# A new order for all operations of a banded attention kernel with a gated output, and its dummy products in pairs

## The chip, the core and the metric

The kernel runs on one core of one Trainium2 chip. The core has five engines that work side by side and each take their own instructions strictly in the order in which the program gives them: TensorE (PE: matrix products; its weight loads are listed apart as PEld), VectorE (DVE), ScalarE (ACT), GpSimd (POOL) and SyncE (SP), whose queue here issues the loads and nearly all stores. They wait for each other through semaphores. The metric is device time in microseconds. Three runs of the kernel before took 269.23, 270.71 and 270.84 us (median 270.71); the profiled execution took 267.36 us, 265.6 us of it between its first and its last instruction (the span).

## What is computed

```python
B, H, S, D = 4, 8, 768, 64; n_sink, window = 4, 128; KT = 5
scores = q @ k.T / sqrt(D)                      # per batch and head
keep   = (key < n_sink) | (0 <= query - key < window)
a      = softmax(where(keep, scores, -1e9))     # row maximum taken off first
x      = (a @ v), heads side by side            # [B, S, 512]
gate   = sigmoid(sum_k conv_w[k] * x[s - 4 + k])   # causal, 5 taps, per channel
out    = (gate * (x @ w_val)) @ w_out
```

The three weights of the second half come as 64-bit floats, which the kernel takes apart itself, as bits, into pairs of 32-bit numbers (a high and a low half); the products of that half are each made from three products of such halves.

## The kernel before, in words

The sequence is cut into 24 steps: 4 batches, 3 blocks of 256 queries, 2 groups of four heads. Steps 0, 1, 6, 7, 12, 13, 18 and 19 are the first blocks of their batches. Two steps (both head groups of one block) make a pair m = 0 to 11, for which the second half is computed. Every piece of work is a named event, `name.step`, and one table of these names, `ORDER`, sets the order in which all engines get their instructions. The function `banded` walks through the table and calls each event. The queues are in order, so the table is the schedule. The names that are spoken of here:

- `kq.s`, `vv.s`: loads of K and Q, and of V, on SP's queue (L234 to L247); three buffers each. `wvl.c`, `wol.c`: loads of a quarter of w_val or w_out, 512 KB (L331); `wva` to `wvf`, `woa` to `wof`: the six stages that take it apart (ACT L135, L149, L154, L181; DVE L138 to L163; POOL L155, L167; for w_val also PE L176 to L178).
- `s0.s`, `s1.s`: the scores of two heads (PE L373) with the mask and the row maximum (DVE L378, and L382 or, in first blocks, L387). `e0`, `e1`: their exponentials (ACT L397). `rec`: one over the row sum, with one instruction on ACT (L403) and one on DVE (L404). `norm`: the normalising (POOL L412 to L421). `tx`, `sk`: transposes on PE (L434, L439). `px` (DVE L463), `py` (ACT L471), `ts` (L447 or L449): they empty the transposes' PSUM.
- `vl.s`, `si.s`: the product with V and that with the sink rows (PE L491, L500), both into the one PSUM tile `xv`. `xc`, `xh`, `hd` (ACT L507, L515, L519): two copies of it, and the 4 columns at its head that the taps reach back to. `xl` (POOL L523): the low half. `c4` (POOL L528), then `c0`, `c1` (DVE L536, four instructions each): the five taps. `vl` of the next step writes `xv` again and waits for `xc`, `xh`, `c0` and `c1`. `th`: the gate's tanh (ACT L541).
- `v0` to `v3` (12 products each, PE L555): x @ w_val in four column blocks, two to a PSUM bank. `y0`, `y1` (ACT L561) copy such a bank out for m = 0 and 1. `g`, `h`, `l` (DVE L574, ACT L580, POOL L584): gate times value, its high half, its low half. `o0` to `o3` (six products each, PE L606): the product with w_out. `t0`, `t1` (ACT L612, then a store): one block of 128 rows to HBM. In the last pair `o2.11` and `o3.11` write their two column halves into two banks, and `t1.11` stores them apart, the second on ACT's own queue.
- `fill`: dummy products of zeros (PE L222), 128 by 512. They write a bank that is free at that point; nothing reads them.

PSUM is tight. `s0`, `s1` and `tx` take turns on two pairs of banks (`pr`): each waits until the user before last has been read, by the exponentials, or in first blocks by DVE, or by `px` and `py`. The products `v`, `o`, `sk`, the w_val stage `wve` and the fills take turns on two banks (`ac`), each of which comes free when `g` (or `y`), `t`, `ts` or `wvf` has read it.

Of the kernel before, what the change touches and what calls it, by code (L numbers as in the profile page):

```python
# [41 lines left out]
sk.1 c1.0 wvf.2 wol.2 e1.3 ts.1 sk.2 px.2 vl.1 rec.3 th.0 woe.1 si.1 xc.1 xh.1 hd.1 wvd.3 s0.4 c4.1 wof.1 c0.1
fill.4g py.2 vv.10 wve.3 woa.2 ts.2 xl.1 woa.3 norm.3 e0.4 c1.1 s1.4 vv.2 wod.1 wvf.3 wob.2 v0.0 wob.3 v1.0 vv.5
tx.3 vl.2 vv.3 y0.0 th.1 v2.0 g0.0 hd.2 py.3 woe.3 h0.0 si.2 e1.4 l0.0 xc.2 v3.0 wod.3 o2.0 px.3 woe.2 y1.0 g1.0
c4.2 rec.4 kq.8 h1.0 wod.2 s0.6 xh.2 e0.6 wof.2 l1.0 s0.5 c0.2 o0.0 wof.3 c1.2 s1.6 o3.0 t1.0 e0.5 o1.0 xl.2 norm.4
sk.3 ts.3 vl.3 si.3 t0.0 kq.7 xc.3 xh.3 tx.4 hd.3 s1.5 sk.4 ts.4 px.4 e1.5 xl.3 v0.1 c4.3 v1.1 rec.5 py.4 v2.1 vv.4
c0.3 y0.1 th.2 c1.3 g0.1 e1.6 v3.1 y1.1 s1.7 s0.7 norm.5 th.3 vl.4 h0.1 l0.1 e1.7 si.4 tx.5 kq.9 rec.6 sk.5 xc.4
o0.1 kq.12 ts.5 g1.1 px.5 hd.4 s1.8 h1.1 o2.1 c4.4 l1.1 xh.4 c0.4 e0.7 o1.1 norm.6 xl.4 o3.1 t0.1 sk.6 vv.7 c1.4
rec.7 py.5 norm.7 tx.6 px.6 vl.5 e1.8 si.5 ts.6 t1.1 py.6 xh.5 xc.5 s0.9 s0.8 xl.5 vv.6 c4.5 sk.7 v0.2 hd.5 ts.7
th.4 e0.9 v1.2 sv.7 c0.5 v2.2 tx.7 c1.5 e0.8 rec.8 sv.6 g0.2 py.7 s1.9 px.7 v3.2 kq.10 th.5 vl.6 h0.2 s1.10 si.6  # L50
e1.9 norm.8 g1.2 xc.6 xh.6 hd.6 l0.2 rec.9 c4.6 tx.8 o0.2 vv.8 h1.2 l1.2 o2.2 xl.6 c0.6 py.8 c1.6 px.8 e1.10 o3.2
scalars s0.12 vl.7 s0.10 norm.9 si.7 t1.2 sk.8 xc.7 tx.9 xh.7 ts.8 hd.7 o1.2 e0.10 c4.7 xl.7 c0.7 v0.3 c1.7 vv.9
v1.3 kq.11 rec.10 vl.8 th.6 si.8 e0.12 px.9 th.7 g0.3 s0.11 xc.8 c4.8 v2.3 xh.8 t0.2 hd.8 py.9 h0.3 sk.9 v3.3 c0.8
vv.11 l0.3 c1.8 s1.11 ts.9 e0.11 g1.3 s1.12 e1.11 h1.3 vl.9 o0.3 norm.10 si.9 tx.10 hd.9 xl.8 l1.3 o2.3 xc.9 kq.13
px.10 rec.11 xh.9 c4.9 kq.15 kq.14 o3.3 e1.12 vv.13 c0.9 o1.3 c1.9 t1.3 sk.10 norm.11 py.10 t0.3 ts.10 s0.13 rec.12
vl.10 xl.9 vv.12 si.10 xh.10 xc.10 tx.11 c4.10 sk.11 hd.10 xl.10 v0.4 ts.11 px.11 th.9 c0.10 e0.13 py.11 sv.12
norm.12 v1.4 v2.4 th.8 c1.10 s1.13 vl.11 tx.12 si.11 g0.4 v3.4 px.12 e1.13 sk.12 rec.13 h0.4 g1.4 py.12 s0.14 xc.11
xh.11 hd.11 vv.16 l0.4 h1.4 c4.11 l1.4 e0.14 kq.18 warm_up s1.14 norm.13 e1.14 ts.12 o2.4 c0.11 o3.4 o0.4 c1.11
s1.18 s0.18 vl.12 si.12 tx.13 vv.18 kq.19 hd.12 th.10 py.13 o1.4 px.13 xl.11 s0.15 t0.4 s1.15 v2.5 t1.4 xc.12 sv.18
xh.12 sk.13 rec.14 c4.12 ts.13 th.11 c0.12 e1.18 c1.12 v3.5 norm.14 v0.5 kq.16 e0.15 e1.15 v1.5 sv.13 g0.5 s0.16  # L60
kq.17 g1.5 vl.13 tx.14 h0.5 si.13 l0.5 o2.5 h1.5 l1.5 xh.13 vv.14 hd.13 rec.15 xc.13 o0.5 c4.13 e0.16 th.12 px.14
o1.5 norm.15 py.14 c0.13 t0.5 o3.5 sk.14 c1.13 tx.15 ts.14 t1.5 py.15 px.15 s1.16 xl.12 vl.14 e0.18 s0.17 hd.14
xl.13 si.14 xc.14 sk.15 kq.20 v2.6 c4.14 xh.14 ts.15 e1.16 v3.6 v0.6 c0.14 rec.16 vv.15 xl.14 th.13 c1.14 e0.17 g1.6
v1.6 g0.6 s1.19 h0.6 norm.16 th.14 l0.6 s0.19 h1.6 kq.21 vl.15 s1.17 l1.6 rec.18 sk.16 si.15 xc.15 ts.16 xh.15 c4.15
tx.16 px.16 o0.6 hd.15 o1.6 c0.15 e1.17 c1.15 rec.17 t0.6 xl.15 py.16 e1.19 th.15 v0.7 v1.7 s0.20 norm.18 vl.16
si.16 xh.16 norm.17 g0.7 tx.17 xc.16 sk.18 v2.7 py.17 h0.7 v3.7 vv.17 c4.16 px.17 hd.16 ts.18 vv.20 c0.16 e0.19 o2.6
g1.7 c1.16 e0.20 h1.7 o3.6 sk.17 ts.17 rec.19 l0.7 kq.23 l1.7 s1.20 e1.20 s0.21 vl.17 o0.7 t1.6 si.17 tx.18 o1.7
norm.19 xc.17 xh.17 c4.17 px.18 hd.17 rec.20 vv.19 py.18 o2.7 c0.17 e0.21 t0.7 xl.16 o3.7 c1.17 tx.19 xl.17 th.17
vl.18 py.19 px.19 s1.21 norm.20 kq.22 si.18 th.16 t1.7 xc.18 tx.20 sk.19 vv.21 px.20 v0.8 c4.18 ts.19 hd.18 sv.19
c0.18 c1.18 v1.8 v2.8 e1.21 v3.8 g0.8 sk.20 py.20 flag ts.20 s1.22 g1.8 xh.18 vl.19 s0.22 h0.8 hd.19 l0.8 si.19 o0.8  # L70
xc.19 xl.18 h1.8 rec.21 c4.19 o2.8 l1.8 xh.19 vv.23 o3.8 c0.19 e1.22 xl.19 o1.8 c1.19 vl.20 s1.23 t1.8 si.20 norm.21
e0.22 tx.21 rec.22 v2.9 xc.20 xh.20 t0.8 c4.20 hd.20 px.21 norm.22 sk.21 ts.21 e1.23 c0.20 th.19 py.21 v3.9 v0.9
c1.20 g1.9 v1.9 th.18 h1.9 vl.21 g0.9 h0.9 s0.23 tx.22 si.21 hd.21 xl.20 l0.9 sk.22 xc.21 o0.9 ts.22 px.22 xh.21
o2.9 vv.22 c4.21 l1.9 c0.21 e0.23 xl.21 py.22 c1.21 o3.9 o1.9 rec.23 vl.22 th.21 t0.9 si.22 norm.23 xc.22 tx.23
px.23 th.20 hd.22 v0.10 c4.22 xh.22 c0.22 t1.9 v1.10 v2.10 g0.10 c1.22 xl.22 h0.10 v3.10 sk.23 py.23 g1.10 l0.10
# [772 lines left out]
```

## Time and profile before

| what | value |
|---|---|
| runs | 269.23, 270.71, 270.84 us |
| profiled execution, its span | 267.36 us, 265.6 us |
| PE busy | 250.7 us (94%) |
| DVE, ACT, POOL busy | 207.1 us (78%), 185.5 us (70%), 177.8 us (67%) |
| TensorE's granted clock | 0.999 of full speed over the span |
| bytes moved | 36.57 MB, mean 138 GB/s |

An engine's busy time counts its own instructions. Matmuls are pipelined and the ends of their records are modelled, so two records can overlap and the busy time of PE says only that it had something in hand. A stretch in which PE is busy all the time can therefore be shortened only by taking work out of it, and this change takes none out.

### The profile page before, as it was taken

The numbers are of one execution on the slowest core, as the hardware profiler recorded it, in microseconds if no ns is written. First come the engines' busy times: TensorE is split into PE (matmuls) and PEld (weight loads), VectorE is DVE, ScalarE is ACT, GpSimd is POOL, SyncE is SP. The second block draws the span as 40 slices with busy tenths as digits, with TensorE's granted clock in tenths as the row PEclk, the third lists the DMA queues.
The fourth block names the chain that finished last, engine by engine and source line by source line (L and its number), as shares of the span: only waits on it lengthen the run. The fifth ranks groups of instructions, "written<-read, shape, count | busy, mean of one in ns | idle before, by whom it ended". The sixth has DMA issues, their size and how long they took to land. (4 is left out here: it accounts for less than half of the span.)

```text
span 265.6 us, 11978 instructions
## 1 busy us (share of the span) xinstructions
PE 250.7 (94%) x4978; PEld 207.6 (78%) x4978; DVE 207.1 (78%) x579; ACT 185.5 (70%) x686; POOL 177.8 (67%) x234
## 2 busy tenths in 40 slices
...
PEclk9999999999999999999999999999999999999999
...
GB/s 203 329 364 236 246 264 39 127 86 265 107 118 168 63 122 84 251 228 116 89 79 232 211 99 207 94 107 165 9 160 174 63 42 102 2 81 2 81 3 88
DMA packets 27548, 36.57 MB, mean 138 GB/s; under 512 B 2272, under 2 KB 24032, under 8 KB 27488
## 3 DMA queue, kind: packets, MB, share of 16 engines
...
q14 instruction: 19, 0.16, 0.2%
q10 hardware_dynamic: 144, 0.13, 0.2%
HBM read 29.45 MB, written 6.29 MB: 135 GB/s over the span
## 5 line engine op out<-in xcount | busy, mean ns | idle before, releaser
L536 DVE SCALAR_TENSOR_TENSOR sg<-xv,cw,sg 128x256 f32<-128x256 f32 x192 | 77.7, 475 | 7.0 <-POOL sg L528 6.3
L412 POOL TENSOR_TENSOR wx<-w,sm 128x512 f32<-128x512 f32 x48 | 49.1, 1043 | 4.6 <-DVE sm L404 4.2
L555 PE MATMUL ac<-xh,wvh 128*128 128x256 f32 x192 | 49.5, 291 | 1.1 <-DVE pr L378 1.1
L584 POOL TENSOR_TENSOR gl<-sg,gh 128x512 fp32r<-128x512 f32 x24 | 30.9, 1291 | 29.1 <-ACT gh L580 29.0
L555 PE MATMUL ac<-xh,wvl 128*128 128x256 f32 x192 | 48.0, 283 | 0.0
L397 ACT ACTIVATE w<-pr,ngm 128x132 f32<-128x132 f32 x128 | 45.7, 369 | 1.7
L373 PE MATMUL pr<-k,q 64*32 64x168 f32 (+2 forms) x1536 | 36.7, 301 | 4.3 <-DMA q<-in_qt_dram 1.4
L528 POOL TENSOR_TENSOR sg<-xt,cw 128x512 f32<-128x512 f32 x24 | 25.5, 1063 | 20.8 <-ACT xt L507 20.7
L606 PE MATMUL ac<-woh,gh 128*128 128x512 f32 (+1 forms) x96 | 39.0, 406 | 0.0
L555 PEld LDWEIGHTS ac<-xh,wvh 128*128 128x128 f32 x192 | 36.9, 192 | 1.7 <-issue 0.5
L555 PEld LDWEIGHTS ac<-xh,wvl 128*128 128x128 f32 x192 | 36.7, 191 | 1.1 <-issue 1.0
L606 PE MATMUL ac<-wol,gh 128*128 128x512 f32 (+1 forms) x96 | 37.3, 388 | 0.0
L491 PE MATMUL xv<-wt,v 64*32 64x192 f32 (+2 forms) x2048 | 36.3, 275 | 1.0 <-PE ac L439 0.8
L606 PE MATMUL ac<-woh,gl 128*128 128x512 f32 (+1 forms) x96 | 37.2, 387 | 0.0
L491 PEld LDWEIGHTS xv<-wt,v 64*32 64x32 f32 x2048 | 33.7, 105 | 3.7 <-issue 1.5
L373 PEld LDWEIGHTS pr<-k,q 64*32 64x32 f32 x1536 | 23.9, 106 | 12.5 <-issue 3.2
L378 DVE COPY_PREDICATED pr<-low,pr 128x256 f32<-128x256 uint8 x48 | 20.3, 423 | 15.4 <-PE pr L373 14.5
L523 POOL TENSOR_TENSOR xl<-xt,xh 128x512 fp32r<-128x512 f32 x24 | 30.8, 1287 | 1.7 <-ACT xh L515 1.6
L555 PE MATMUL ac<-xl,wvh 128*128 128x256 f32 x192 | 30.9, 283 | 0.0
L555 PEld LDWEIGHTS ac<-xl,wvh 128*128 128x128 f32 x192 | 26.5, 192 | 0.0
L397 ACT ACTIVATE w<-sx,ngm 128x132 f32<-128x132 f32 x64 | 25.0, 400 | 1.9 <-DVE ngm L387 1.9
L397 ACT ACTIVATION_READ_ACCUMULATOR w<-pr,ngm 128x1 f32 x128 | 26.0, 203 | 0.0
...
## 6 DMA issues: line engine op xcount, KB each, us to landing
...
q<-in_qt_dram SPq DMA_DIRECT2D x23, 256.0 KB, 5.3
out_dram<-osb SPq DMA_DIRECT2D x23, 256.0 KB, 2.6
...
v<-in_vt_dram SPq DMA_DIRECT2D x8, 256.0 KB, 3.9
...
```

The costliest lines, as they stand in the source:

```text
L373: nc.tensor.matmul(ss[e * QB:(e + 1) * QB, j, c * n + x0:c * n + x1], q[js, g, (4 * c + e) * QB:(4 * c + e + 1) * QB], k[js, g, (2 * c + e ...
L378: nc.vector.copy_predicated(sv[:, :, :, :D], low[:, None, None, :].to_broadcast([P, 2, 2, D]), sv[:, :, :, 2 * HB:])
L397: nc.scalar.activation(out=w[:, g, j, c], in_=sx[:, j, c, :PK], func=AF.Exp, scale=0.125 if steps[s][1] else -1.0, bias=ngm[:, g, j, c:c + ...
L412: nc.gpsimd.tensor_tensor(out=t[:, n].rearrange("p c h x -> p h c x"), in0=w[:, :, :, at], in1=sm.to_broadcast([P, 4, 2, D]), op=ALU.mult)
L491: nc.tensor.matmul(acc[r0:r0 + QB, g, x0 + h * D:x0 + (h + a1 - a0 + 1) * D], v[js, g, n, e * QB:(e + 1) * QB], t[js, n % 2, n // 2, g, a0 ...
L523: nc.gpsimd.tensor_tensor(out=half(xls, s, "xl", F32R), in0=xts[s], in1=half(xhs, s, "xh", F32R).bitcast(F32), op=ALU.subtract)
L528: nc.gpsimd.tensor_tensor(out=half(sg, s, "sg", F32), in0=xts[s], op=ALU.mult, in1=cw[:, g, KT - 1:].to_broadcast([P, 2, PQ]))
L536: nc.vector.scalar_tensor_tensor(out=g, in0=x, scalar=a, in1=g, op0=ALU.mult, op1=ALU.add)
L555: nc.tensor.matmul(acc[:, h], a[:, kc, cs], x[:, kc], start=(n == 0), stop=(n == 11))
L584: nc.gpsimd.tensor_tensor(out=gl, in0=g, in1=gh.bitcast(F32), op=ALU.subtract)
L606: nc.tensor.matmul(to, a[:, kc, ts], x[:, kc, cs], start=(kc + n == 0), stop=(kc + n == 5))
```

## The change

The table is replaced by another with the same events, but for the fills: ten groups of four products before, twenty groups of two now (of twenty-four names that the new code defines), 40 products either way. Loads stay on SP's queue. No operation changes its shape, its engine or its buffers' number.

```diff
 ORDER = """
-load_conv masks signs fill.4a wvl.0 kq.0 wva.0 wvl.1 conv_weights wvb.0 s0.0 wvc.0 wvd.0 s1.0 wve.0 wvl.2 e0.0 wva.1
-wva.2 blanks fill.4f kq.1 wvb.1 kq.2 e1.0 wvc.1 wvb.2 fill.4l fill.4h s0.1 rec.0 wvc.2 vv.0 wvf.0 s1.1 s1.2 wol.0
...
-ts.23 th.22 vl.23 h1.10 si.23 xc.23 l1.10 xh.23 xl.23 hd.23 o2.10 o0.10 o3.10 o1.10 t1.10 v0.11 t0.10 c4.23 v1.11
-v2.11 c0.23 g0.11 c1.23 h0.11 v3.11 l0.11 o0.11 th.23 g1.11 h1.11 l1.11 o2.11 o1.11 o3.11 t0.11 t1.11
+masks fill.2g fill.2h wvl.0 fill.2t signs load_conv kq.0 wvl.1 wva.0 conv_weights wvl.2 kq.1 kq.2 fill.2b wvb.0
+wvd.0 s0.0 wvc.0 wva.1 e0.0 s1.0 wve.0 vv.0 wol.0 fill.2r wva.2 wvb.1 fill.2c blanks e1.0 wvb.2 fill.2k s0.1 wvc.1
...
+o1.10 xh.23 hd.23 t0.10 o3.10 xl.23 v0.11 t1.10 th.22 v1.11 v2.11 c0.23 c1.23 g0.11 h0.11 th.23 l0.11 v3.11 g1.11
+o2.11 o0.11 h1.11 l1.11 o3.11 t1.11 o1.11 t0.11
 """
...
-    for n in "abcdefghijklmnop":
-        events["fill.4" + n] = busy, (4,)
+    for n in "abcdefghijklmnopqrstuvwx":
+        events["fill.2" + n] = busy, (2,)
```

Three places show how the instructions move; the line numbers of the changed kernel are higher by one.

VectorE, early in the program, from the masking of step 1's transposes (`px.1`) to the taps of step 0 (`xv` is the product with V, `wo_t` belongs to a quarter of w_out). Before:

```order
L463 TENSOR_TENSOR wt<-pr_86,prev 128x2x2x64
L404 RECIPROCAL sm<-sm 128x8
L536 SCALAR_TENSOR_TENSOR sg<-xv,cw,sg 128x256 x4
L378 COPY_PREDICATED pr_87<-low,pr_87 128x2x2x64
L382 TENSOR_REDUCE ngm<-pr_87 128x4
L138 TENSOR_SCALAR wo_t<-wo_p 128x512
L140 SCALAR_TENSOR_TENSOR wo_t<-wo_p,wo_t 128x512
```

And now:

```order
L405 RECIPROCAL sm<-sm 128x8
L464 TENSOR_TENSOR wt<-pr_86,cur 128x2x4x64
L464 TENSOR_TENSOR wt<-pr_86,prev 128x2x2x64
L537 SCALAR_TENSOR_TENSOR sg<-xv,cw,sg 128x256 x8
L379 COPY_PREDICATED pr_87<-low,pr_87 128x2x2x64
L383 TENSOR_REDUCE ngm<-pr_87 128x4
L139 TENSOR_SCALAR wo_t<-wo_p 128x512
```

All eight taps of step 0 now run in one piece, ahead of the mask and maximum of `s1.3` and of a stage of the weights, which stood between `c0.0` and `c1.0`.

TensorE, from the sink product of step 8 to the product with V of step 9, the first row of each group of products. Before:

```order
L500 MATMUL xv<-skt,vh 128x256 x2
L373 MATMUL pr_87<-k,q 32x168 x16
L555 MATMUL ac_93<-xh,wvh 128x256
L439 MATMUL ac_92<-ident,skb_106 128x128
L373 MATMUL pr_86<-k,q 32x168 x16
L373 MATMUL pr_87<-k,q 32x104
L491 MATMUL xv<-wt,v 32x64 x8
```

And now:

```order
L501 MATMUL xv<-skt,vh 128x256 x2
L556 MATMUL ac_92<-xh,wvh 128x256
L440 MATMUL ac_93<-ident,skb_106 128x128
L374 MATMUL pr_86<-k,q 32x168 x16
L374 MATMUL pr_87<-k,q 32x104
L492 MATMUL xv<-wt,v 32x64 x8
```

The scores `s0.11` no longer stand between `si.8` and `vl.9`; `v2.3`, `v3.3`, `sk.9`, `s1.11` and `s1.12` still do.

SyncE's queue of loads, from the first quarter of w_out to the V of step 1 (`raw` are the weights' tiles). Before:

```order
L331 DMA raw<-in_w_out_dram 128x1024
L234 DMA k<-in_kt_dram 128x2x408
L236 DMA q<-in_qt_dram 128x2x256
L331 DMA raw<-in_w_val_dram 128x4x256
L243 DMA v<-in_vt_dram 128x2x256
```

And now:

```order
L332 DMA raw<-in_w_out_dram 128x1024
L235 DMA k<-in_kt_dram 128x2x408
L237 DMA q<-in_qt_dram 128x2x256
L332 DMA raw<-in_w_out_dram 128x1024
L332 DMA raw<-in_w_val_dram 128x4x256
```

A second quarter of w_out (`wol.1`) has come in ahead of the last quarter of w_val (`wvl.3`).

At the end of the table, as the diff's last lines show, `t0.11` and `t1.11` have changed places: the block that is stored whole (128 by 512, on SP's queue) is now behind the one that is stored in two halves, and `o1.11` is the last group of products.

## Rows read from the trace of the kernel before

**Rows 1.** The page: busy time by engine, and the granted clock in 40 slices.
```profile
PE 250.7 (94%) x4978; PEld 207.6 (78%) x4978; DVE 207.1 (78%) x579; ACT 185.5 (70%) x686; POOL 177.8 (67%) x234
PEclk9999999999999999999999999999999999999999
```

**Rows 2.** Busy time by stretch: us from the start, length, then each engine (instructions).
```profile
0.00:10.00 10.00, 7.56 (x78) 2.90 (x78) 7.23 (x40) 4.83 (x14) 5.36 (x19) 1.00 0.75 234
10.00:20.00 10.00, 8.03 (x133) 4.29 (x133) 9.16 (x36) 9.65 (x38) 5.65 (x7) 1.00 1.06 364
20.00:30.00 10.00, 8.23 (x195) 5.19 (x194) 9.63 (x22) 9.61 (x42) 9.38 (x14) 1.00 0.79 252
30.00:40.00 10.00, 9.15 (x172) 5.79 (x171) 9.90 (x22) 9.24 (x31) 8.83 (x10) 1.00 0.74 240
250.00:266.00 16.00, 10.06 (x73) 9.26 (x72) 2.94 (x6) 3.26 (x6) 2.58 (x2) 0.96 0.16 55
```

**Rows 3.** Timeline of TensorE: start, length, what, idle time before it.
```profile
10.01 2.76 PE L222 MATMUL ac<-zero 128*128 128x512 bf16 x12
13.15 1.29 PE L373 MATMUL pr<-k,q 64*32 64x104 f32 x64 [0.38 <-DMA q<-in_qt_dram]
15.61 0.81 PE L373 MATMUL pr<-k,q 64*32 64x168 f32 x32 [1.17 <-DVE ngm L387]
...
33.66 1.25 PE L491 MATMUL xv<-wt,v 64*32 64x192 f32 x64 [0.81 <-PE ac L439]
...
55.81 1.59 PE L491 MATMUL xv<-wt,v 64*32 64x64 f32 x96
```

**Rows 4.** Waits of TensorE: us in total, times, longest.
```profile
PE ac L555 <- DVE pr L378: 1.1, 1, 1.1
PE pr L373 <- issue: 0.6, 1, 0.6
PE pr L373 <- ACT w L397: 0.4, 1, 0.4
```

**Rows 5.** The chain that ended last: start, length, what; pieces of it.
```profile
148.26 1.53 ACT w L397 x8
...
158.88 0.73 PE pr L373 x32
...
162.38 5.74 PE ac L555 x48
```

**Rows 6.** Timeline of VectorE: taps of step 0, `c0.0` and `c1.0`.
```profile
27.84 1.66 DVE L536 SCALAR_TENSOR_TENSOR sg<-xv,cw,sg 128x256 f32<-128x256 f32 x4
...
31.90 1.65 DVE L536 SCALAR_TENSOR_TENSOR sg<-xv,cw,sg 128x256 f32<-128x256 f32 x4
```

**Rows 7.** Timeline of ScalarE: `wva.3`, `hd.0`, `xh.0`, `wvc.3`, then `wvf.1` and `wvf.2`.
```profile
21.97 0.66 ACT L135 ACTIVATE wv_p<-raw 128x512 f32<-128x512 f32 x1
...
25.93 0.20 ACT L519 ACTIVATE xv<-none 128x8 f32<-128x8 f32 x1
...
29.74 0.57 ACT L515 ACTIVATE xh<-xv 128x512 fp32r<-128x512 f32 x1
30.22 0.66 ACT L154 ACTIVATE wv_p<-raw 128x512 f32<-128x512 uint32 x1
30.79 1.05 ACT L181 ACTIVATE wvl<-ac 128x512 fp32r<-128x512 f32 x2
```

**Rows 8.** The weights' raw tiles: time from issue to landing of their loads.
```profile
DMA to landing us min/median/max: 3.9/5.9/8.5
```

**Rows 9.** Timeline, all engines, behind the sink product of step 8: `xc.8`, `c4.8`.
```profile
104.71 0.60 ACT L507 ACTIVATE xt<-xv 128x512 f32<-128x512 f32 x1 [1.38 <-PE xv L500]
...
105.39 1.04 POOL L528 TENSOR_TENSOR sg<-xt,cw 128x512 f32<-128x512 f32 x1 [4.90 <-ACT xt L507]
```

**Rows 10.** Timeline of VectorE, the same place: `c0.8` and `c1.8`.
```profile
106.60 3.21 DVE L536 SCALAR_TENSOR_TENSOR sg<-xv,cw,sg 128x256 f32<-128x256 f32 x8
```

**Rows 11.** Timeline of the end: copies of the last blocks out of PSUM on ScalarE.
```profile
258.67 0.60 ACT L612 ACTIVATE osb<-ac 128x512 f32<-128x512 f32 x1 [2.65 <-PE ac L606]
...
260.10 0.38 ACT L612 ACTIVATE osb<-pr 128x256 f32<-128x256 f32 x1 [0.28 <-PE pr L606]
```

**Rows 12.** DMA issues: queue, count, size, median us from issue to landing.
```profile
out_dram<-osb SPq DMA_DIRECT2D x23, 256.0 KB, 2.6
...
out_dram<-osb ACTq DMA_DIRECT2D x1, 128.0 KB, 2.1
```

More of the change, by code (lines that the diff above doesn't have):

```diff
@@ L42 @@
[L42 to L75, printed above, removed]
-ts.23 th.22 vl.23 h1.10 si.23 xc.23 l1.10 xh.23 xl.23 hd.23 o2.10 o0.10 o3.10 o1.10 t1.10 v0.11 t0.10 c4.23 v1.11
@@ L77 @@
-v2.11 c0.23 g0.11 c1.23 h0.11 v3.11 l0.11 o0.11 th.23 g1.11 h1.11 l1.11 o2.11 o1.11 o3.11 t0.11 t1.11
+masks fill.2g fill.2h wvl.0 fill.2t signs load_conv kq.0 wvl.1 wva.0 conv_weights wvl.2 kq.1 kq.2 fill.2b wvb.0
+wvd.0 s0.0 wvc.0 wva.1 e0.0 s1.0 wve.0 vv.0 wol.0 fill.2r wva.2 wvb.1 fill.2c blanks e1.0 wvb.2 fill.2k s0.1 wvc.1
+rec.0 kq.3 wvc.2 fill.2d s1.1 norm.0 fill.2i wvf.0 s1.2 wvd.1 wve.1 sv.0 fill.2l e0.1 woa.0 e1.2 tx.0 wol.1 fill.2j
+wob.0 py.0 fill.2f e1.1 fill.2e wvl.3 woe.0 wvf.1 px.0 rec.1 sk.0 s0.2 wva.3 ts.0 wol.2 s0.3 vl.0 fill.2m wod.0 vv.1
@@ new lines @@
+e0.2 si.0 vv.5 vv.2 wof.0 wvb.3 xc.0 norm.1 rec.2 xh.0 c4.0 wvc.3 xl.0 hd.0 fill.2o wvd.2 sv.1 tx.1 norm.2 wve.2
+kq.4 e0.3 fill.2s fill.2a px.1 py.1 c0.0 c1.0 sk.1 ts.1 woa.1 s1.3 wob.1 th.0 vl.1 fill.2n wvf.2 si.1 woe.1 e1.3
+s1.4 kq.6 hd.1 tx.2 xc.1 xh.1 xl.1 vv.6 wod.1 c4.1 rec.3 wvd.3 v0.0 wof.1 px.2 c0.1 v1.0 woa.2 wol.3 fill.2q norm.3
+fill.2p c1.1 e1.4 py.2 wve.3 woa.3 y0.0 sk.2 th.1 ts.2 wob.2 g0.0 wvf.3 wob.3 s0.4 vl.2 h0.0 v2.0 si.2 e0.4 kq.7
+woe.3 v3.0 tx.3 l0.0 y1.0 py.3 sk.3 woe.2 xh.2 ts.3 kq.5 g1.0 xc.2 px.3 wof.2 wod.2 hd.2 vv.3 h1.0 c4.2 s0.6 o0.0
```

34 lines of the change are left out of this document (31 added, 3 removed).

## Prediction

> **What bounds the kernel now.** I read the page's busy times first, then the busy time by stretch, then TensorE's own waits, then the chain that ended last, and at last the timeline wherever one of these pointed.
>
> [...] The stretches say where the other 14.9 us lie [rows 2]: in the first four tens it is busy for 7.56, 8.03, 8.23 and 9.15 us, 7.0 us short; from 250 us on for 10.06 of the 15.6 us left, 5.5 us short. The rest, 2.4 us, is spread over 210 us, and its three longest waits there are 1.1, 0.6 and 0.4 us [rows 4]. So the program has a head of 40 us, in which TensorE waits for others, a body, in which it does not, and a tail behind its last product. The change does the same products in another order; in the body nothing can be won but those three waits, 2.1 us.
>
> What holds the head is seen in the same rows: VectorE is busy for 9.16, 9.63 and 9.90 us and ScalarE for 9.65, 9.61 and 9.24 of each ten between 10 and 40 us. Both take the weights apart while they serve the first steps. TensorE's largest waits there end with their work: 1.17 us on VectorE at 15.61, and 0.81 us ahead of `vl.1` at 33.66 [rows 3]. The second is put down to TensorE's own transpose; but the last of step 0's taps, which `vl.1` waits for too, ended at 31.90 + 1.65 = 33.55 [rows 6], and I take that for the one that came last.
>
> The chain that ended last lies on TensorE from 149.8 us on; just ahead of that stand three sets of exponentials on ScalarE, of some 1.53 us each [rows 5].
>
> **The change, part by part.** Durations are of the profiled execution, 267.36 us (1.8 us around its span). It is 3.35 us under the median of the three runs, 270.71; I add my sum to the one and carry it to the other.
>
> *The first 13 us: nothing.* The big loads of the first steps keep their order; the conv weights' small load only changes places with the first quarter of w_val. TensorE's fills change in number of places, not in sum, and stand where it waits anyway.
>
> *Head, on VectorE: a gain.* `vl.1` waits for the last of step 0's taps. `c0.0` ended at 27.84 + 1.66 = 29.50 and `c1.0` began at 31.90 [rows 6]; the 2.40 us between them held `s1.3` and half of a weight stage, which now stand behind. Against that, `c0.0` needs `hd.0`, which ended at 25.93 + 0.20 = 26.13. On ScalarE there are now ahead of it one `wvf` more (half of 1.05, 0.52), `xh.0` (0.57) and `wvc.3` (0.66) [rows 7], less `sv.1`, which I leave out as small. And `wva.3` waits for its load. That load took up to 8.5 us [rows 8], and its tile was read at 21.97 us with no wait named [rows 7]; now 512 KB more go ahead, which at the 252 to 364 GB/s of these stretches [rows 2] are 1.4 to 2.0 us. ScalarE would get there 0.5 us later than before, so it stands for 0.9 to 1.5 us at most; since landing had some margin that the trace does not show, I take 0.5. `hd.0` then ends at 26.13 + 0.52 + 0.57 + 0.66 + 0.5 = 28.4, and `c1.0` at 28.4 + 3.2 (eight taps in one piece, as in [rows 10]) = 31.6. It ended at 31.90 + 1.65 = 33.55 before. So `vl.1` can start 1.9 us earlier.
>
> TensorE does not gain 1.9 us by it: `tx.2`, `sk.2` and some fills stood ahead of `vl.1` and are now behind it. The next place with equal product work ahead in both orders is `vl.3`, at 55.81 us [rows 3]. Between the two, ScalarE gives part of it back: the first products with w_val are moved up, so that `xh.1` and the bank's copy `y0.0` are waited for earlier in ScalarE's queue, and one more set of exponentials (`e1.4`, 1.53 by [rows 5]) stands ahead of `y0.0`. The bounds are +2.3 us (1.53 and 0.8 of load wait, nothing hidden) and −1.9 (nothing given back). I take −0.7, near the middle and a little to the gain, since both engines' work up to `vl.3` is the same but for its order.
>
> *Body.* Step 9 has less cover. From the end of `si.8` a copy (0.60) [rows 9], `c4.8` (1.04) and eight taps (3.21) [rows 10] must pass before `vl.9`, 4.85 us, some 5.1 with the hand-overs that the rows' starts show (104.71 to 109.81). On TensorE there stood before four groups of scores' and products' work in between; `s0.11` (0.73 by [rows 5]) is moved ahead, and what is left is `v2.3` and `v3.3` (a quarter of 5.74 each [rows 5], 2.87), `s1.11` and `s1.12` (at most 0.73 each) and a transpose: some 4.3 to 4.4. TensorE waits for **0.75 us** at `vl.9`. Against that, `s0.16` waited for 0.4 us on ScalarE [rows 4], behind the three sets of exponentials; these are now spread among the products of pair 5, so 0.4 goes. What is late next there is nothing that I can name. Sum +0.35, between −2.1 (all three waits go, `vl.9` hidden) and +3 (three more places as short of cover as `vl.9`).
>
> Two of the three waits, 1.1 and 0.6 us, I leave standing. The one put down to issue has no releaser, and the longer names an instruction whose result the waiting product does not read [rows 4]. Both look like TensorE's stream of instructions arriving late, which goes on whatever the order. [...]
>
> *Loads.* SP's queue still issues everything in order, and a load can stand behind a store that waits. Loads of K, Q and V keep some 6 us or more of product work between the release of their buffer and their use in both orders, so I put them at nothing; what covers them is that work, and a load that came one wait later would cost what is missing of it.
>
> *Tail: a loss.* Behind the last product stood a copy of 128x256 (0.38) and a store of 128 KB on ACT's queue (2.1). Now it is a copy of 128x512 (0.60) [rows 11] and a store of 256 KB on SP's (2.6) [rows 12]: 0.22 + 0.5 = **+0.7 us**, between +0.3 and +1.0. The last products themselves are the same.
>
> Sum: −0.7 + 0.35 + 0.7 = **+0.35 us**: 267.7 for a profiled execution, and 271.1 against the median.
>
> **Rivals.**
>
> *ScalarE takes over the head (slower).* For it: ScalarE is as full there as VectorE [rows 2], it waits for the later load and stands ahead of nearly every release of a bank; when its `rec.2` comes late, VectorE stands too, and the gain at `c1.0` is lost. Against it: its idle time in that head is not nil, and half of what is moved up was ready before. It decides if the last quarter of w_val lands after some 23.5 us. Price: the 2.3 us of the bound above in place of the gain, and the forecast's 0.35 and 0.7: +3.35, so 274.1 us.
>
> *All waits of the body go, and the head keeps its whole gain (faster).* −1.9 in the head, −2.1 in the body, +0.7 at the end: −3.3, so 267.4. [...] Against it: `vl.9`.
>
> [...]
>
> **How the numbers follow.** Three runs lie 1.6 us apart, so 1% (2.7 us) is about what can be told from no change. Forecast, within 1%: 0.49. Faster rival: 0.25; half of a gain would not leave the 1%, but it stands for other gains in the head that I cannot price. ScalarE's head: 0.22. The clock, or a load come late: 0.04. So faster 0.25, same 0.49, slower 0.26. The forecast's own range is 269 to 273; the range for 8 in 10 takes in both rivals, 267 to 275.
>
> **What would show it.** `c0.0` and `c1.0` in one piece, ending near 31.6 us; `vl.3` near 55.1; a wait of TensorE for VectorE's taps at `vl.9` of some 0.75 us; a last store that lands 0.7 us later behind the last product. I am wrong if `vl.3` starts before 53.5 or after 58 us, if a granted clock under 1.00 stands in any slice before the end, or if waits of over 1 us on loads appear in the body.

## The result, and the profile after

Twenty runs of each kernel were made side by side. The median of the changed kernel is 271.31 us (270.32 to 273.38), that of the one before 269.07 us (265.97 to 272.06): 2.24 us or 0.8% more. The ratio of the two, new to old, is 1.012, with a 95% interval of 1.0093 to 1.0146. (The ratio leaves out runs over 1.5% above the fastest of their kernel, here six of the twenty before and none of the changed ones, and so comes out higher than that of the medians.) So the change makes the kernel slower, by 2 to 4 us. The forecast time, 271.1 us, lies 0.2 us from the measured one, but by luck: the three runs that it was carried to had a median of 270.71 us, 1.6 above that of the twenty. The change itself was forecast at +0.35 us, and that was too little. Between the two profiled executions it is +2.96 us: 270.32 against 267.36.

Where these 2.96 us lie is read from equal places in both programs. The product with V of step 3 (`vl.3`) starts 1.52 us later (57.33 for 55.81), the last product ends 0.60 later than that (at 262.18 for 260.07), the rest of the span is 0.29 longer (5.82 for 5.53), and 0.56 lie around the span.

The page of the changed kernel, busy times and granted clock, beside [rows 1]:

```profile
PE 251.9 (94%) x4978; PEld 207.1 (77%) x4978; DVE 210.4 (79%) x579; ACT 185.6 (69%) x686; POOL 178.5 (67%) x234
PEclk9999999999999999999999999999999999999997
```

The head by tens of microseconds, beside [rows 2] (TensorE's busy time is the first after the length, ScalarE's the fourth; the clock is the third from the end):

```profile
0.00:10.00 10.00, 7.90 (x82) 3.24 (x82) 7.49 (x42) 3.71 (x7) 5.28 (x19) 1.00 0.73 225
10.00:20.00 10.00, 7.76 (x130) 3.64 (x131) 8.30 (x35) 9.95 (x40) 5.04 (x7) 1.00 1.06 374
20.00:30.00 10.00, 7.51 (x162) 4.21 (x161) 8.78 (x19) 8.93 (x37) 8.93 (x12) 1.00 0.80 266
30.00:40.00 10.00, 8.70 (x176) 6.21 (x177) 9.78 (x20) 9.81 (x40) 9.60 (x12) 1.00 0.55 176
```

TensorE is 8.13 us short of full there, 7.03 before; the loss sits between 20 and 40 us. TensorE's waits, beside [rows 4]:

```profile
PE pr L374 <- DMA q<-in_qt_dram: 2.4, 2, 1.7
PE ac L607 <- DVE skt L450: 1.6, 1, 1.6
PE pr L208 <- DVE warm L760: 1.2, 1, 1.2
PE ac L223 <- issue: 1.2, 1, 1.2
PE pr L374 <- ACT sm L404: 1.1, 1, 1.1
```

All three waits of the body, 1.1, 0.6 and 0.4 us, are gone. Two that I had not seen coming have appeared: 1.6 us on VectorE's L450, and 1.2 us of "issue". TensorE's timeline says where (beside [rows 3]; the first row is the wait for K and Q ahead of `s0.1`, the last the first product of `o2.5`):

```profile
13.43 0.75 PE L374 MATMUL pr<-k,q 64*32 64x104 f32 x32 [1.73 <-DMA q<-in_qt_dram]
...
25.11 0.39 PE L223 MATMUL ac<-zero 128*128 128x512 bf16 x1
26.67 0.38 PE L223 MATMUL ac<-zero 128*128 128x512 bf16 x1 [1.17 <-issue]
26.97 0.39 PE L501 MATMUL xv<-skt,vh 64*128 64x256 f32 x2
27.29 0.61 PE L223 MATMUL ac<-zero 128*128 128x512 bf16 x2
27.83 0.71 PE L435 MATMUL pr<-ident,wx 64*128 64x64 f32 x16
...
33.00 1.25 PE L492 MATMUL xv<-wt,v 64*32 64x192 f32 x64 [0.45 <-DVE sg L537]
...
57.33 0.94 PE L492 MATMUL xv<-wt,v 64*32 64x64 f32 x48
...
109.81 0.75 PE L374 MATMUL pr<-k,q 64*32 64x104 f32 x32 [0.30 <-ACT w L398]
110.72 1.58 PE L492 MATMUL xv<-wt,v 64*32 64x64 f32 x96 [0.16 <-PE pr L374]
...
157.14 0.51 PE L607 MATMUL ac<-woh,gh 128*128 128x512 f32 x1 [1.64 <-DVE skt L450]
```

The pair of dummy products ahead of the sink product (`si.0`, 26.97) is torn apart: the second stands 1.17 us with nothing named, and `tx.1` comes at 27.83 us, 2.0 later than before.

VectorE's eight taps of step 0, beside [rows 6], are now in one piece:

```profile
29.52 3.22 DVE L537 SCALAR_TENSOR_TENSOR sg<-xv,cw,sg 128x256 f32<-128x256 f32 x8
```

What makes `o2.5` wait at 157 us is seen on VectorE. There `flag`, nine tiny instructions that I had passed over, now stands ahead of L450, which empties the bank that `o2.5` needs:

```profile
152.74 0.16 DVE L105 CAST nw_f<-nw_raw 128x4 f32<-128x4 int32 x1
152.93 1.00 DVE L107 TENSOR_SCALAR nw<-nw_f 128x2 f32<-128x2 f32 x1
153.97 0.96 DVE L108 TENSOR_TENSOR nw<-nw,nw_f 128x2 f32<-128x2 f32 x1
154.96 0.97 DVE L109 TENSOR_SCALAR nw<-nw 128x2 f32<-128x2 f32 x1
155.97 0.16 DVE L110 TENSOR_TENSOR nw<-nw,nw_f 128x2 f32<-128x2 f32 x1
...
156.68 0.41 DVE L450 TENSOR_TENSOR skt<-ac,blk 128x256 fp32r<-128x256 f32 x1
```

Instructions on 128 by 2 numbers last 0.16 us or 1 us. GpSimd's timeline of the same stretch tells which:

```profile
152.86 1.05 POOL L529 TENSOR_TENSOR sg<-xt,cw 128x512 f32<-128x512 f32 x1
153.86 2.04 POOL L413 TENSOR_TENSOR wx<-w,sm 128x512 f32<-128x512 f32 x2
```

L107 ends at 153.93, as GpSimd's L529 does (153.91); L108 and L109 end at 154.92 and 155.93, as the two of L413 do (154.91 and 155.91). Each of these three lasts until GpSimd's running instruction is through, and the next then stands behind the next of GpSimd's. (Not all nine do: in the run flag_late below the two of L113, on 128 by 1, took 0.15 us each while GpSimd's L529 ran.) What holds these three, and not the others, no run here shows.

### The profile page after: what moved, and what is told of

It reads as the page before. It is cut to its first block, busy times and chain, and to the rows that moved or that the text cites. A ratio compares the mean times of both kernels' runs of the same rounds, so it can differ in the third digit from the quotient of the medians.

```text
span 268.0 us, 11977 instructions
## 1 busy us (share of the span) xinstructions
PE 251.9 (94%) x4978; PEld 207.1 (77%) x4978; DVE 210.4 (79%) x579; ACT 185.6 (69%) x686; POOL 178.5 (67%) x234
## 4 chain that ended last, share of the span: by engine, by line
PE 81%; ACT 8%; POOL 4%; DVE 2%; issue 2%; DMA 1%; SPq 0%; POOLq 0%
PE ac L556 25%; PE ac L607 24%; PE xv L492 12%; PE pr L374 10%; PE pr L435 4%; ACT w L398 3%; PE xv L501 3%; PE ac L440 1%; DMA craw<-in_conv_w_dram 1%; POOL xl L524 1%; ACT wv_p L155 1%; POOL wx L413 1%; POOL wv_f L156 1%; ACT wvh L150 1%; PE ac L223 1%
## 5 line engine op out<-in xcount | busy, mean ns | idle before, releaser
L413 POOL TENSOR_TENSOR wx<-w,sm 128x512 f32<-128x512 f32 x48 | 49.3, 1047 | 7.9 <-DVE sm L405 7.6
L529 POOL TENSOR_TENSOR sg<-xt,cw 128x512 f32<-128x512 f32 x24 | 25.0, 1043 | 30.5 <-ACT xt L508 30.4
L585 POOL TENSOR_TENSOR gl<-sg,gh 128x512 fp32r<-128x512 f32 x24 | 31.0, 1295 | 18.1 <-ACT gh L581 18.0
L374 PE MATMUL pr<-k,q 64*32 64x168 f32 (+2 forms) x1536 | 37.3, 301 | 4.2 <-DMA q<-in_qt_dram 2.4
L508 ACT ACTIVATE xt<-xv 128x512 f32<-128x512 f32 x24 | 14.3, 598 | 17.0 <-PE xv L501 16.7
```

The costliest lines, as they stand in the source:

```text
L374: nc.tensor.matmul(ss[e * QB:(e + 1) * QB, j, c * n + x0:c * n + x1], q[js, g, (4 * c + e) * QB:(4 * c + e + 1) * QB], k[js, g, (2 * c + e ...
L413: nc.gpsimd.tensor_tensor(out=t[:, n].rearrange("p c h x -> p h c x"), in0=w[:, :, :, at], in1=sm.to_broadcast([P, 4, 2, D]), op=ALU.mult)
L508: nc.scalar.activation(out=t, in_=accs[s][:, :, KT - 1:], func=AF.Copy)
L529: nc.gpsimd.tensor_tensor(out=half(sg, s, "sg", F32), in0=xts[s], op=ALU.mult, in1=cw[:, g, KT - 1:].to_broadcast([P, 2, PQ]))
L585: nc.gpsimd.tensor_tensor(out=gl, in0=g, in1=gh.bitcast(F32), op=ALU.subtract)
```

## The experiments

**Three single parts put back, and all three.** Each is one name moved in the table, but for the head as a whole.

```diff
 e0_first
-wva.1 e0.0 s1.0
+e0.0 wva.1 s1.0
 flag_late
-o1.5 flag c4.13
+g0.8 flag ts.20
 before_head: everything up to vl.3 in the order of the kernel before
 three_back: e0_first, flag_late, and at the end
-o3.11 t1.11 o1.11 t0.11
+o1.11 o3.11 t0.11 t1.11
```

> The changed kernel with one pair of names swapped: ScalarE does step 0's exponentials e0.0 before it takes up the second quarter of w_val (wva.1), as in the kernel before. Theory A (ScalarE stands for a load): ScalarE idles 1.54 us up to 10.02 because wva.1 now stands first and its 512 KB have not landed; with the swap e0.0 starts near 8.8 in place of 10.59, TensorE's first product with V (vl.0) 0.8 us earlier (23.1 for 23.9), and the product with V of step 3 (vl.3) 0.5 to 0.8 us earlier than its 57.33; span 267.3, about 0.7 us under the changed kernel, ratio to the kernel before near 1.009. Rival B (VectorE or GpSimd hold the head): vl.0 moves, vl.3 by less than 0.2 us, ratio stays at 1.012. Rival C (the load only looks late because another wait is hidden under it): ScalarE stands as long in front of the next instruction and vl.0 does not move.

Ratio 1.0058 (1.0021 to 1.0095), median 271.33 us; `vl.0` at 24.64, `vl.3` at 57.65. Theory A fell. The ratio is lower than the changed kernel's because the kernel before came out slower beside this run (median 269.50); the run's own median is the changed kernel's, 271.31. Between the groups of runs the kernel before has medians from 268.52 to 270.12, so differences of half a per cent between ratios of two groups say little. In the changed kernel ScalarE's wait is

```profile
10.02 0.67 ACT L136 ACTIVATE wv_p<-raw 128x512 f32<-128x512 f32 x1 [1.54 <-POOL skb L319]
```

and ScalarE's timeline in this run:

```profile
9.43 0.39 ACT L398 ACTIVATE w<-sx,ngm 128x132 f32<-128x132 f32 x1
10.64 0.68 ACT L136 ACTIVATE wv_p<-raw 128x512 f32<-128x512 f32 x1 [0.73 <-DMA raw<-in_w_val_dram]
12.10 0.68 ACT L136 ACTIVATE wv_p<-raw 128x512 f32<-128x512 f32 x1 [0.77 <-DMA raw<-in_w_val_dram]
```

`e0.0` runs early, at 8.24, and ScalarE then waits for both quarters of w_val all the same: the loads set its pace in either order. And `si.0` came at 27.28 whatever `vl.0` did. One row more from this run, TensorE's stretch behind a wait of 2.57 us for K and Q:

```profile
14.00:18.00 4.00, 3.96 (x72) 1.41 (x72) 2.81 (x16) 3.83 (x13) 3.01 (x3) 0.57 1.09 380
```

The granted clock has a mean of 0.57 of full speed over these 4 us, and is 0.50 from 15 to 17 us.

> The changed kernel with the nine small VectorE instructions of the event flag moved back to where the kernel before has them, ahead of ts.20; TensorE's order is untouched. Theory A: the one wait of 1.64 us that TensorE has at 157 us (o2.5, on VectorE's L450, which stood behind flag) goes as a whole and nothing comes in its place, since TensorE has no idle time of over 0.3 us behind it; span 266.4, ratio near 1.006. Rival B (the flag only hid another shortage): the wait shrinks to 0.5 to 1 us on another VectorE or ScalarE instruction of steps 13 and 14. Rival C: the flag, which took 4 us in place of 1.6 here, takes as long at the new place and a wait of over 1 us stands there instead: ratio stays 1.012.

Ratio 1.0075 (1.0035 to 1.0115), median 271.75 us. The wait at `o2.5` shrank from 1.64 to 0.3, and another came up at the new place, as rival C had it:

```profile
216.54 1.58 PE L492 MATMUL xv<-wt,v 64*32 64x64 f32 x96 [1.77 <-DVE sg L537]
```

There `flag` took 207.17 to 210.63, 3.5 us, beside three of GpSimd's instructions. In the kernel before, at the same name but with GpSimd idle for the first 0.9 us of it, it took 2.4, 0.94 of that in the one instruction that ran to the end of one of GpSimd's.

> The changed kernel, but everything up to the product with V of step 3 (vl.3) in the order of the kernel before; from there on the changed order. Theory A (of the loss of 2.1 us up to the last product, 1.5 arise in the head): vl.3 back at 55.8 (57.33 in the changed kernel, 55.81 in the one before), span 266.5, ratio 1.005 to 1.007; the wait of 1.64 us at o2.5 stays. Rival B (the body takes back what the head gives, since other engines set its pace): vl.3 earlier, but the step-23 product with V no earlier than its 243.1 less 0.5 us, ratio over 1.009. Rival C (the head cannot be had without the old body): waits of over 1 us directly behind vl.3.

`vl.3` at 55.95: the order up to there makes 1.4 us, which is theory A's number. But the whole came out worse: span 272.1 (in a run of 274.11 us; the median of the six is 272.79), ratio 1.0101 (1.0039 to 1.0163). The gain was lost directly behind `vl.3`, as rival C had it; TensorE's timeline there:

```profile
58.51 0.27 PE L435 MATMUL pr<-ident,wx 64*128 64x64 f32 x1
60.49 0.66 PE L435 MATMUL pr<-ident,wx 64*128 64x64 f32 x15 [1.70 <-issue]
```

and by stretches:

```profile
56.00:60.00 4.00, 2.79 (x132) 2.16 (x132) 2.18 (x11) 3.39 (x12) 2.27 (x6) 1.00 0.97 297
62.00:64.00 2.00, 2.00 (x11) 2.00 (x11) 2.00 (x5) 1.97 (x12) 0.00 (x0) 0.50 1.03 342
```

Within a set of 16 transposes TensorE stands for 1.70 us while the loads fill the DMA engines (share 0.97), and behind it the granted clock is 0.50 of full speed (62 to 64 us). `vl.5` is then 2.8 us later than in the kernel before. The loads are so thick there because of the join itself: `kq.7`, `vv.6` and `kq.8` come close behind `vl.3` in this table, and in the same stretch the share is 0.51 in the kernel before and 0.47 in the changed one (57 to 61 us). So this run shows what the order up to `vl.3` costs, and not what the old head would be worth with the new body.

> The changed kernel with three things put back as in the kernel before: e0.0 ahead of wva.1, flag ahead of ts.20, and at the very end o1.11 ahead of o3.11 with t0.11 and then t1.11, whose second half goes out on ScalarE's own queue. Theory A (three separate losses that add): 0.7 + 1.6 + 0.3, span 265.4, ratio 1.000 to 1.003. Rival B (only the flag's wait is on the path): span 266.4, ratio near 1.006. Rival C (the waits only move): ratio over 1.009.

Ratio 1.0046 (1.0010 to 1.0082), median 271.12 us, span 268.1. The losses did not add up as theory A had it, since two of the three edits were not what I took them for. The stretch behind the last product was shorter, 5.0 us for 5.8; but over the five profiles that end as the kernel before does it lies between 4.9 and 5.9, and over the nine that end as the changed one does between 5.8 and 6.1, so 0.5 us is the difference of their means and a single pair tells little.

**What "issue" is.** I counted all the instructions that TensorE had begun when such a stand came (a time in which it is idle with nothing named): its weight loads and products, and also the hundred others, nearly all of which only wait for semaphores; without them the pattern below is not there. In the kernel before, two of the body's waits come after 1985 and 4033 of them, in the changed kernel the one at 26.67 after 705, in before_head after 1985 and 3265: each 193 more than a multiple of 256. The page lists 41 transfers of 16 KB on the instruction queue for 10,060 instructions, 245 to a transfer. So TensorE stands where one transfer's instructions end and the next is not there. The starts of these transfers, in the timeline's count of time (the expectations give them 0.13 us less), against the end of the stand:

```
kernel             transfer  TensorE on  between  stand
before, 59 us        56.78      59.51      2.73    0.62
before, 106 us      103.74     106.50      2.76    1.10
after                24.21      26.67      2.46    1.17
before_head          57.88      60.48      2.60    1.70
loads_late           25.19      27.59      2.40    1.99
flag_free            24.52      27.00      2.48    1.66
mended               26.53      28.85      2.32    3.62
hold, 36 us          33.59      35.81      2.22    2.02
hold_all             24.37      27.27      2.90    1.74
spread               23.42      26.32      2.90    1.74
```

TensorE goes on 2.2 to 2.9 us after the transfer has begun. In the first 40 us of most of these it began as the data loads ran out, as in the changed kernel at 24.21, with the DMA engines' share at 1.06, 0.80 and 0.32 in the microseconds from 22, 23 and 24. That was the theory of the next runs.

```diff
 loads_late
-wva.3 ts.0 wol.2 s0.3 ... si.0 vv.5 vv.2 ... kq.4 e0.3
+wva.3 ts.0 s0.3 ... si.0 vv.2 ... kq.4 wol.2 vv.5 e0.3
 flag_free
-o1.5 flag c4.13
+v2.11 flag c0.23
 b_loads (the kernel before)
-e1.2 wvl.3 py.0 ... wol.1 si.0 ... wol.3 ... wol.2
+e1.2 wol.1 wvl.3 wol.2 py.0 ... si.0 ... wol.3
 mended: e0_first, loads_late, flag_free, and
-kq.18 ... kq.14
+kq.14 kq.18
```

> The changed kernel with two loads taken out of the crowd on SyncE's queue: wol.2 (512 KB) and vv.5 (384 KB), which went out at 15.5 and 17.3 us, now stand behind kq.4, which goes out at 25.5 to 27.5 us. Nothing else moves. Theory A (TensorE's instructions come late behind data loads): in the changed kernel TensorE stands 1.17 us before 26.67 with no releaser named, and the transfer of its next 16 KB of instructions began only at 24.08, just when the loads' backlog ended (DMA share 1.06, 0.80, 0.32 in the stretches from 22, 23 and 24 us). With 0.9 MB less ahead the backlog ends near 21.7, that transfer starts before 22.5, the stand goes, the sink product si.0 starts near 25.4 in place of 26.98, the transposes tx.1 near 26.3 (they wait for GpSimd then) in place of 27.84, and vl.3 near 56.0 in place of 57.33; span 266.7 to 267. Rival B (si.0 waits for a result of another engine, GpSimd or ScalarE, that the profile does not name): si.0 stays at 26.9 to 27.0 and vl.3 at 57.3. Rival C (the gain at 26 us is eaten by woa.2 or a later product that now waits for the moved load): si.0 early, vl.3 over 57.

Ratio 1.0135 (1.0073 to 1.0197). The edit did the opposite of what I meant: with `vv.5` gone, `vv.2` found a buffer, no longer stood in SyncE's way, and let `kq.4` and `wol.2` out at 17.5 and 19.3 us. The loads lasted a microsecond longer, the transfer began at 25.19, and the stand grew to 1.99 us: the theory's arithmetic with the other sign.

> The changed kernel with the event flag put where VectorE and GpSimd are both idle: directly ahead of c0.23, where VectorE stands for 5.85 us from 244 to 249.84 us. Theory A (each small VectorE instruction of flag waits until the GpSimd instruction that is running has ended, and what stands behind flag waits with it): the nine instructions take 1.6 to 1.8 us in place of 3.9 (152.74 to 156.75), each under 0.25 us; the wait of 1.64 us at o2.5 goes, none of 1.8 us comes up at vl.21 as it did with flag ahead of ts.20; last product 1.6 us earlier; ratio to the kernel before lower than the changed kernel's by 0.006. Rival B (the order is short of something else there): a wait of over 0.5 us at o2.5 stays, named for another instruction. Rival C (flag's instructions are slow by themselves): they take over 3 us here too.

Ratio 1.0018 (0.9981 to 1.0055), median 269.41 us: of the 1.2% one per cent is gone. By the medians it is 1.9 us, the 1.64 us of `flag` and a little more. VectorE's timeline:

```profile
242.68 0.16 DVE L105 CAST nw_f<-nw_raw 128x4 f32<-128x4 int32 x1
242.88 0.17 DVE L107 TENSOR_SCALAR nw<-nw_f 128x2 f32<-128x2 f32 x1
243.08 0.16 DVE L108 TENSOR_TENSOR nw<-nw,nw_f 128x2 f32<-128x2 f32 x1
243.28 0.17 DVE L109 TENSOR_SCALAR nw<-nw 128x2 f32<-128x2 f32 x1
```

With GpSimd idle the nine take 1.6 us, the wait at `o2.5` is gone, and none came up elsewhere. Theory A holds.

> The kernel before, with the loads of w_out moved up as the change has them: wol.1 ahead of wvl.3, wol.2 just behind it. Nothing else moves. Theory A (the loads' backlog delays TensorE's instructions): the backlog lasts to about 24.5 us in place of 22; the transfer of TensorE's next instructions that began at 21.98 begins at 24 or later, the wait ahead of tx.1 at 25.80 grows from 1.1 to about 2 us with no releaser named, or tx.1 starts at 26.6 or later; wva.3, which waits for wvl.3, starts at most 1 us later. vl.3 0.5 to 1 us later than 55.81. Rival B: the instructions' transfer starts near 22 us again and tx.1 near 25.8; then the loads' place costs nothing.

The transfer began at 24.19 in place of 22.11, `tx.1` came at 26.72 (25.80), `vl.3` at 56.23 (55.81); ratio 1.0028 (0.9967 to 1.0088). The transfer and `tx.1` moved as theory A had it, in the other kernel and with nothing but loads moved; `vl.3` a little less. What the loads cost on average the ratio does not settle: the ten runs lie between 267.55 and 275.00 us with a median of 272.20 (268.87 for the kernel before beside them), and the profile, of 268.51 us, is one of the short ones.

> The changed kernel with four single names moved: e0.0 ahead of wva.1, wol.2 and vv.5 behind kq.4, flag ahead of c0.23, and the load kq.14 ahead of kq.18 (TensorE waited 0.75 to 0.81 us for kq.14's data at 132 us in three of the variants; it went out at 126.2 behind kq.18, which is used 6 us later). Theory A (four separate losses): head 1.3, flag 1.6, kq.14 0 to 0.8: span 264.3 to 265.2, ratio to the kernel before 0.994 to 1.000. Rival B (only the flag pays): span 266.4, ratio 1.004 to 1.006. Rival C (waits only move): ratio over 1.008.

Ratio 1.0013 (0.9971 to 1.0055). In the profile the head is 4 us worse, with a stand of 3.62 us, for the reason of loads_late; this is the longest of the twelve runs, 272.73 us where their median is 269.71, so most runs lost less. The rest holds what was expected: no wait for K and Q at 132 us, where the eight variants that leave `kq.14` behind `kq.18` had 0.3 to 0.8 us, and no wait at `o2.5`.

**Holding the loads back rightly.**

```diff
 hold: flag_free, and
-wva.3 ts.0 wol.2 s0.3 ... kq.4 e0.3
+wva.3 ts.0 s0.3 ... kq.4 wol.2 e0.3
 hold_all: hold, e0_first, kq.14 ahead of kq.18, the end of three_back, and
-fill.2k s0.1
+fill.2k fill.2d fill.2i fill.2l s0.1
 hold_nofill: hold without the dummy products of the table
 spread: hold_all, and wol.1 behind vv.2, kq.6 behind wol.3
```

> The kernel with flag ahead of c0.23 (flag_free) and one load more moved: wol.2 behind kq.4, with vv.5 left where it is. In loads_late the fourth V tile no longer stood in SyncE's way, so kq.4 and wol.2 went out at 17.5 and 19.3 us and the backlog grew; here the next V load still waits for its buffer until 25 us and holds kq.4 and wol.2 behind it. Theory A (TensorE's next instructions arrive 2.3 to 2.8 us after their transfer begins, and it begins when the loads' backlog ends): 512 KB less are 1.4 us at some 370 GB/s; the transfer begins near 22.9 us (24.39 in flag_free), the stand ahead of si.0 falls from 1.66 us to 0.2 or none, si.0 near 25.5 (27.31), tx.1 near 26.4 (28.16; it then waits for GpSimd), vl.3 near 56.2 (57.65); ratio 0.005 under flag_free's 1.0018. Rival B (no effect of loads on instructions): si.0 within 0.3 us of 27.0. Rival C: si.0 early, but woa.2, which reads wol.2, or a later step waits, and vl.3 over 57.2.

Ratio 1.0005 (0.9966 to 1.0043), median 269.37 us. TensorE's timeline:

```profile
25.79 0.38 PE L501 MATMUL xv<-skt,vh 64*128 64x256 f32 x2
...
27.28 0.72 PE L435 MATMUL pr<-ident,wx 64*128 64x64 f32 x16 [0.57 <-POOL skb L416]
...
35.81 0.39 PE L223 MATMUL ac<-zero 128*128 128x512 bf16 x1 [2.02 <-ACT w L398]
```

The transfer began at 22.54, the stand ahead of `si.0` went, and `si.0` came 1.5 us earlier than in flag_free: theory A's first half. But the next boundary, at 35.8 us, now had a stand of 2.02 us, and `vl.3` came at 58.24. The moved load and its neighbours were under way up to some 33 us, and the transfer began at 33.59; that this one load makes it is not shown, since hold_all has it at the same place without this stand. (The profile names ScalarE there. The 2.22 us since the transfer began speak for the instructions, and so does the count: 957, four short of 193 past a multiple of 256, in a trace that lacks six of TensorE's records.) Rival C, in another place than I had looked for it.

> hold, and four things more put back: e0.0 ahead of wva.1; the load kq.14 ahead of kq.18; the three pairs of dummy products d, i and l ahead of s0.1, so that twelve stand there again; and at the end o1.11, o3.11, t0.11, t1.11 as in the kernel before. Theory A: no fall of the granted clock between 13 and 18 us (seen in three of eight profiles with six products there), no wait for K or Q at 132 us, the end 0.3 us shorter behind the last product: 0.5 to 1.0 us under hold and 0.2 to 0.8% under the kernel before. Rival B (the head is set by the instruction transfer and by GpSimd, so that e0.0 and the dummy products do not matter): vl.3 as in hold, 0.3 us from the end alone. Rival C: the extra dummy products delay s0.1 and vl.0 by 0.5 us and vl.3 with it.

Ratio **0.9951** (0.9918 to 0.9984), median 267.81 us against 270.12: faster than the changed kernel, and by half a per cent faster than the kernel before, which is as much as that one's own medians differ between groups of runs. No fall of the clock in the head (1.00 of full speed in each ten up to 40 us), no wait for K and Q at 132 us, and 4.9 us behind the last product where hold has 5.9 (spread, with the same end, has 5.9 as well). Which of the four edits the gain comes from was not taken apart. `vl.3` is at 57.64, with a stand of 1.74 us ahead of `si.0` that hold did not have.

> hold without any of the forty dummy products in the order (they write nothing that is read; the six at the very start stay). [...] Rival B (they hold the clock, and without it the head grows): vl.3 2 us or more later. Rival C (they are a cost, by 0.1 to 0.2 us a pair where TensorE is full, and they shift where its stream of instructions breaks): vl.3 0.5 us or more earlier than hold's.

Ratio 1.0093 (1.0057 to 1.0130), median 271.94 us, 2.6 over hold. Yet `vl.3` is earlier, at 57.10. TensorE's timeline shows 1.9 us of the loss far behind the head, at 113 and 173 us, where hold has no dummy products either:

```profile
113.03 0.51 PE L492 MATMUL xv<-wt,v 64*32 64x128 f32 x18 [1.06 <-issue]
...
173.48 0.27 PE L492 MATMUL xv<-wt,v 64*32 64x64 f32 x5 [0.86 <-issue]
```

Both come 193 past a multiple of 256 (4289 and 6849). Eighty instructions fewer in the head moved each boundary behind it, and two now fall into products with V, where 18 products take 0.51 us (one of 128 by 512 takes 0.39). That is rival C's second half, with a cost where it expected a gain.

> hold_all with two more loads moved: wol.1 (512 KB) behind vv.2, so that it goes out at 26 us in place of 14, and kq.6 (664 KB, used at 49.5 us) behind wol.3, out at 37 us in place of 27.5. Theory A (TensorE asks for its next instructions on entering a page of them, near 21.3 us here; asked for while data loads are queued they take until the queue is through and 2.3 to 2.8 us more): the loads end near 21.2 us in place of 22.6, the transfer starts before 22.5 (24.24 in hold_all), the stand of 1.74 us ahead of si.0 falls under 0.4, si.0 near 25.6 (27.28), tx.1 near 26.7 (28.13); the next one, at 30 to 33 us, is not late either since 664 KB less are under way; vl.3 56.0 to 56.7 (57.64); ratio 0.991 to 0.993. Rival B (TensorE's instructions come when they come, and the loads only happen to end then): the transfer starts at 24 us again, si.0 at 27. Rival C (the stand moves on to a later page, as in hold, where 2.0 us came up at 35.7): tx.1 early, vl.3 over 57.2, ratio 0.995.

Ratio 0.9972 (0.9939 to 1.0005), median 267.52 us. `vl.3` at 56.69, as theory A had it, but not by its mechanism: everything from `s0.1` on is a microsecond earlier than in hold_all, since K and Q landed earlier in this run, and the stand ahead of `si.0` is 1.74 us again. The DMA engines' share was 0.43 from 21 to 22 us and 0.05 from 22 to 23, and the transfer began at 23.42. So the end of the loads is not what starts it. Other transfers say so too: those at 31.22 in hold_all and at 30.38 here began with the share near 1.

What the traces do show is when TensorE passed the boundary *before* the one that each transfer serves. In the changed kernel, where hardly a load was under way then, transfers began soon behind that: at 35.31 behind 34.11, at 43.83 behind 43.41, at 79.29 behind 78.57. Under loads they began later: at 17.21 behind 13.46, at 24.21 behind 21.47, at 30.65 behind 26.67; here at 23.42 behind 20.67, and in hold, where loads went out as the boundary was passed, at 33.59 behind 25.79; though not always: the changed kernel's transfer at 122.78 began close behind 122.08, with the share near 1. In b_loads, where only loads were moved, the 1.00 us of the kernel before (22.11 behind 21.10) became 2.64 (24.19 behind 21.55). So in these traces a transfer follows the passing of the boundary before, and loads under way then can hold it back, in b_loads by 1.6 us and in hold by 7; **what sets whether and by how much stays open**.

## Why the prediction was right and wrong

- *The first 13 us, "nothing": wrong, without a price.* `wva.1` stands ahead of `e0.0`, and ScalarE waited 1.54 us up to 10.02 for it. e0_first shows that it would have waited for the loads anyway. TensorE's 1.73 us for K and Q at 13.43 are the 0.38 of the kernel before and the six dummy products that no longer stand there, half of 2.76 us [rows 3].
- *Head, VectorE's taps: right in kind, 1.1 us off in time.* `c0.0` and `c1.0` ran in one piece and ended at 29.52 + 3.22 = 32.74, forecast 31.6. `hd.0` did not wait for w_val's last quarter, as I had it, but came at 29.25 behind the late `si.0`. `vl.1` started 0.65 us earlier than before, not 1.9.
- *Head, what is given back: **the step that failed**.* I had put the net at −0.7 us at `vl.3`, between −1.9 and +2.3; it is +1.52. before_head shows that the order up to `vl.3` makes it. The rival in which ScalarE takes over the head had a price nearer to that, but its condition did not come: `wva.3` was read at 23.02 us with no wait. A part is the late instructions at 25 us, which hold took away and met again at 36 us; how the rest divides between ScalarE and the boundary was not settled, as no variant with this head but spread got `vl.3` under 57 us.
- *Body, the two odd waits: wrong.* I left 1.1 and 0.6 us standing "whatever the order". They were stands at boundaries, and these fall on other products in another order: both went, and one came at 26.67. At most boundaries no such stand is seen: of the 39 in each trace, TensorE's next instruction began over 0.4 us behind the one ahead of it at three in the kernel before (25.44 us, put down to GpSimd, 59.51 and 106.50) and at one in the changed kernel (26.67); the stands measured in all runs were of 0.6 to 3.6 us.
- *Body, `vl.9` and `s0.16`: right.* `s1.12` and `vl.9` waited 0.30 + 0.16 us, forecast 0.75, behind taps that ended at 110.63; the 0.4 us at `s0.16` went.
- *Body, not in the sum: `flag`, 1.64 us.* The order moved it from step 20 to step 14, where GpSimd is busy and a bank is wanted. The prediction does not name it: nine tiny instructions stood at nothing, and nothing was named that covers them. It is the largest term of all, and flag_free gives it back: 1.0018 in place of 1.012. This term, which the sum did not have, and the head's, which it had with the wrong sign, make up the loss. The forecast +0.35 us lay within the 1% that I had called no change; the measured 0.8 to 1.2% lies at its edge.
- *Body as a whole:* forecast +0.35, measured +0.60, the sum of −2.1, +1.64, +0.46 and 0.6 that I cannot place.
- *Loads, "nothing": nearly.* The changed profile shows no wait for K and Q in the body, but eight variants with the same body do, 0.3 to 0.8 us at `s1.14`; `kq.14` goes out 5.5 us ahead of its use, where it had 19 before, and where I had counted on 6 or more. With it ahead of `kq.18` the wait was gone in all three profiles.
- *Tail: right in kind,* +0.29 us where 0.7 stood in the sum, and 0.5 between the means of all profiles with either end.
- *The clock, 0.04 of the forecast together with a late load: it fell in variants, and does not make the loss.* With six dummy products in place of twelve TensorE waited 1.7 to 2.6 us for K and Q, and there the granted clock fell from 1.00 of full speed to 0.50 in four of eight profiles, the changed kernel's not among them. With the fall `vl.0` came at 24.01 to 24.64, without it at 23.63 to 23.90, and where nothing else was changed ahead of it `si.0` at 27.01 with it (flag_late) and at 26.97 without (the changed kernel): TensorE had time to spare there. Of the twenty runs of the changed kernel the ten with the higher mean clock have a median of 271.1 us, the others 271.5, so the clock does not make the loss. In before_head TensorE had no time to spare; a granted clock of 0.50 over 3.4 us makes 1.7 us, as an estimate of what that fall cost.
